# The first k in two hardware transfers, and the identity built on POOL behind the third load

## The chip, the cores and the metric

One core of one Trainium2 chip. The metric is the device time of one execution, in microseconds (us). Engines are named as the profile names them: PE multiplies matrices (PEld is its weight load), DVE, ACT and POOL are the elementwise engines, and SP only issues transfers here. A transfer goes either through a "hardware" queue (issued on SP or ACT) or through the "software" queue (issued on POOL). A name ending in "q", as in POOLq, is the sequencer of that engine.

## The reference

```python
# q, k, v: (8, 12, 448, 64) f32; w_in: (768, 2048); w_out: (2048, 768)
scores = q @ k.transpose(0, 1, 3, 2) / sqrt(64)
attn   = np.maximum(scores, 0.0) ** 2 / 448
x      = (attn @ v).transpose(0, 2, 1, 3).reshape(3584, 768)
h      = x @ w_in
out    = (0.5 * h * (1 + erf(h / sqrt(2)))) @ w_out
```

## The kernel before

The kernel works through eight batches of twelve heads; a batch is three head groups of four. For the first batches, q and k are transposed on PE against an identity matrix. From batch 2 on, DVE packs them (`pk`, `pq`) and transfers issued on SP transpose them (`kT`, `qT`). All instructions go out in a recorded order, so that no engine chooses at run time.

The start: the first k and q come as f32 through two hardware queues, the identity is made by DVE and POOL, and PE spins on zeros until data come.

```python
    nc.scalar.dma_start(k32, kv_view(k, 0, 0, 1))
    nc.sync.dma_start(q32, q_view(0, 0, 1, 0, HC))
    zero = const.tile([128, 128], BF16, tag="zero", name="zero")
    V.memset(zero, 0.0)
    V.memset(ident, 0.0)
    nc.gpsimd.affine_select(
        out=ident, in_=ident, compare_op=mybir.AluOpType.not_equal, fill=1.0,
        base=0, pattern=[[-1, 128]], channel_multiplier=1,
    )
    # ... a warming activation on ACT ...
    for _ in range(SPIN):                      # 45
        nc.tensor.matmul(spin[:, 0, :128], zero, zero, start=True, stop=True)
```

The gate: a POOL instruction that copies one column of each of the four transposed parts of q. Its purpose, as the code reads, is to hold POOL, which issues the large loads, until the transposes of the batch have landed.

```python
        def fn(e):
            nc.gpsimd.tensor_copy(gate, get_T(b)[0][:, 0, ::KC])
```

Behind the gate of batch 2 stand the second and third load of `w_out` and then the next loads of k and q:

```python
    def load_wout(kf):
        w = moe_w_out.rearrange("(kf p) d -> p kf d", p=128)
        nc.gpsimd.dma_start(wout_sb[:, kf, :], w[:, kf, :])
```

Of the kernel before, what the change touches and what calls it, by code (L numbers as in the profile page):

```python
# [12 lines left out]
B, H, S, D = 8, 12, 448, 64  # L13
# [5 lines left out]
NK = S // KB  # L19
# [37 lines left out]
K_CUT = 4  # L57
# [1 line left out]


ORDER = """
G0 G1 G2 G3 G4 G5 A10 D13 G6 A16 P11 P14 G7 D12 A15 P17 G8 D18 P21 P39 D22 P33 P36 A34 D40
P19 D20 A37 P23 G9 P42 P48 D24 P54 A43 D35 A49 P51 D44 P25 D38 A52 D41 G117 A55 D53 P45 D50
A26 D47 A46 P57 D56 P69 P66 A58 D70 P27 G118 A67 P29 D59 P63 G119 A28 D71 P60 A64 G120 D68
P78 D61 A62 P75 A79 D65 P81 P31 D30 A76 D80 P96 G121 D32 A97 P72 D77 G122 A82 D98 P129 G123
# [140 lines left out]
def kernel(  # L206
# [9 lines left out]
    nc = tc.nc  # L216
# [24 lines left out]
    k32 = natpool.tile([128, 2, NK * D], F32, tag="pk", name="k32")  # L241
# [9 lines left out]
    def q_view(b, g0, g1, c0, c1):  # L251
        qq = q[b, 4 * g0 : 4 * g1].rearrange("h (p c) d -> p h (c d)", c=NC)
        return qq[:, :, c0 * D : c1 * D]
# [7 lines left out]
    def kv_view(t, b, g0, g1):  # L261

        return t[b, 4 * g0 : 4 * g1].rearrange("h s d -> (h s d)").rearrange(
            "(x p f) -> p x f", p=128, f=NK * D
        )
# [27 lines left out]
    ident = const.tile([128, 128], BF16, tag="ident", name="ident")  # L293
# [10 lines left out]
    V, A = nc.vector, nc.scalar  # L304
# [12 lines left out]
    sch = Scheduler({"w": 3, "a": NA, "f": 2, "osb": 3})  # L317
# [412 lines left out]
    def f2(b):  # L730
        tiles = range(0, 3) if b % 2 == 0 else range(3, 7)
        return [(2.6, add_f2(b // 2, t, n)) for t in tiles for n in range(2)]

    def mix(a, b):

        a, b = list(a), list(b)
        r, n = [], len(a) + len(b)
        na = len(a)
        for i in range(n):
            if a and (not b or (na - len(a) + 1) * n <= (i + 1) * na):  # L740
                r.append(a.pop(0))
            else:
                r.append(b.pop(0))
        return r
# [12 lines left out]
    def slots(first, last):  # L757
# [10 lines left out]
        return out + [[("AV", done)]]  # L768


    nc.scalar.dma_start(k32, kv_view(k, 0, 0, 1))
    nc.sync.dma_start(q32, q_view(0, 0, 1, 0, HC))
    zero = const.tile([128, 128], BF16, tag="zero", name="zero")
    V.memset(zero, 0.0)  # L774
    V.memset(ident, 0.0)
    nc.gpsimd.affine_select(
        out=ident, in_=ident, compare_op=mybir.AluOpType.not_equal, fill=1.0,
        base=0, pattern=[[-1, 128]], channel_multiplier=1,
    )
    warm = const.tile([128, 1], F32, tag="warm", name="warm")  # L780
    V.memset(warm, 0.0)

# [127 lines left out]
    x1, x2 = f1(B - 1), f2(B - 2)  # L910
    for _, o in x2[:1] + mix(x1, x2[1:]) + f2(B - 1):
        pe_q.append(o)
    sch.run({"PE": pe_q, "POOL": pool_q})
# [1 line left out]
_INS = ['q', 'k', 'v', 'moe_w_in', 'moe_w_out']  # L915
# [26 lines left out]
```

## Time and profile before

| what | value |
|---|---|
| time | 392.37 us, median of 3 runs (392.07 to 392.56) |
| span of the profiled run | 391.1 us |
| PE busy | 381.2 us (97%) |
| ACT, DVE, POOL busy | 200.1, 189.9, 45.7 us |
| first transposes on PE | 6.02 us |
| last landing that holds PE back | 86.3 us |

PE bounds the kernel over the whole.

The transfer queues, too, can be read from the page (packets, MB, share of 16 engines):

```profile
q10 hardware_dynamic: 304, 0.48, 0.3%
```

This is the queue of the first k: 256 of its packets are k (1792 bytes each), and 16 of 4 bytes tell that the transfer is complete. The other 32 belong to a small store that ACT issues at the end of the kernel. The q beside it is on another hardware queue.

### The profile page before, as it was taken

To read this page: it belongs to the slowest core of one execution; us is meant where nothing else is said; L and a number is where in the kernel's file an instruction comes from. 1 tells how busy PE (TensorE), PEld (TensorE's weight loads), DVE (VectorE), ACT (ScalarE), POOL (GpSimd) and SP (SyncE) were. 2 spreads that over 40 slices of the span, in tenths; PEclk is the share of its full clock that TensorE was granted. 3 is DMA by queue.
4 is the path that set the end of the run, shared out by engine and by line. 5 is a ranking of instruction groups with operands and counts; after the bars stand their busy time and mean duration, and the time that the engine had idled before them with its cause. 6 is when DMAs were issued, how large, how long until landed. Compare 5 with 4: busy or idle time off the path is not lost.

```text
span 391.1 us, 7974 instructions
## 1 busy us (share of the span) xinstructions
PE 381.2 (97%) x3437; PEld 211.6 (54%) x3437; DVE 189.9 (49%) x350; ACT 200.1 (51%) x304; POOL 45.7 (12%) x69
## 2 busy tenths in 40 slices
PE   8799999998999999999999999999999999999996
PEld 7576554454555555555555555555555555555563
DVE  3999952457636444644555346545355352110121
ACT  4988855743536554565734466366536645222200
POOL 8665304000200200020000200000000000000000
PEclk9999999999999999999999999999999999999999
DMA  9999998999997691689129961380112011100132
GB/s 176 195 203 204 197 175 112 210 202 152 182 188 134 126 178 42 130 138 169 42 65 159 128 125 42 76 148 2 40 23 60 2 42 40 42 13 29 40 80 82
DMA packets 69523, 42.94 MB, mean 110 GB/s; under 512 B 37744, under 2 KB 65904, under 8 KB 69488
## 3 DMA queue, kind: packets, MB, share of 16 engines
q0 software_dynamic: 30512, 22.47, 38.4%
q1 hardware_dynamic: 38672, 19.49, 24.1%
q8 instruction: 27, 0.44, 0.5%
q10 hardware_dynamic: 304, 0.48, 0.3%
q14 instruction: 8, 0.07, 0.0%
HBM read 45.61 MB, written 11.01 MB: 145 GB/s over the span
## 4 chain that ended last, share of the span: by engine, by line
PE 85%; DMA 7%; DVE 4%; SPq 1%; ACT 1%; POOL 1%; issue 0%; POOLq 0%
PE pso L687 36%; PE psh L644 33%; PE ps L535 8%; PE pav L597 7%; DMA nq<-in_q_dram 5%; DVE a_sq L556 2%; SPq L498 1%; DMA q<-in_q_dram 1%; DVE a_sq L549 1%; DMA qT<-pq 1%; ACT a_sq L547 1%; PE tp L465 1%; PE tp L437 0%; DVE osb L308 0%; DVE pq L397 0%
## 5 line engine op out<-in xcount | busy, mean ns | idle before, releaser
L644 PE MATMUL psh<-xT,win_sb 128*128 128x448 bf16 (+1 forms) x804 | 154.3, 344 | 0.0
L687 PE MATMUL pso<-wout_sb,h_sb 128*128 128x384 bf16 (+2 forms) x896 | 151.7, 326 | 0.6 <-DVE osb L308 0.6
L547 ACT ACTIVATE a_sq<-ps 128x896 bf16<-128x896 f32 (+1 forms) x141 | 123.2, 914 | 48.9 <-PE ps L535 48.8
L556 DVE TENSOR_TENSOR a_sq<-a_sq 128x896 bf16<-128x896 bf16 (+1 forms) x169 | 100.5, 618 | 53.7 <-ACT a_sq L547 53.5
L656 ACT ACTIVATE h_sb<-psh 128x448 bf16<-128x448 f32 x128 | 70.0, 547 | 98.5 <-PE psh L644 98.5
L687 PEld LDWEIGHTS <-h_sb 128*128 128x128 bf16 x896 | 86.2, 98 | 63.0 <-issue 6.3
L644 PEld LDWEIGHTS <-win_sb 128*128 128x128 bf16 x804 | 76.2, 98 | 70.4 <-issue 9.5
L308 DVE COPY osb<-pso 128x384 f32<-128x384 f32 (+2 forms) x56 | 31.2, 557 | 89.6 <-PE pso L687 89.6
L535 PE MATMUL ps<-qT,kT 64*64 64x448 bf16 (+1 forms) x756 | 47.0, 336 | 2.6 <-DVE a_sq L549 0.9
L549 DVE TENSOR_SCALAR a_sq<-ps 128x896 bf16<-128x896 f32 x28 | 30.4, 1090 | 35.9 <-PE ps L535 35.6
L597 PE MATMUL pav<-a_sq,v_sb 64*64 64x448 bf16 (+1 forms) x756 | 37.3, 330 | 1.0 <-ACT a_sq L547 0.4
L535 PEld LDWEIGHTS <-kT 64*64 64x64 bf16 x756 | 18.4, 105 | 24.2 <-issue 19.2
L597 PEld LDWEIGHTS <-v_sb 64*64 64x64 bf16 x756 | 21.3, 107 | 13.6 <-issue 2.9
L308 DVE CAST xT<-pav 128x448 bf16<-128x448 f32 (+1 forms) x29 | 16.3, 567 | 9.2 <-ACT xT L310 4.6
L310 ACT CAST xT<-pav 128x448 bf16<-128x448 f32 (+1 forms) x25 | 12.4, 495 | 15.5 <-PE pav L597 9.8
L510 POOL COPY gate<-qT 128x4 bf16<-128x4 bf16 x5 | 0.9, 187 | 157.4 <-DMA qT<-pq 157.4
L257 POOL DMA_DIRECT2D nq<-in_q_dram x14 | 11.6, 829 | 2.0 <-DMA win_sb<-in_moe_w_in_dram 0.8
L359 POOL DMA_DIRECT2D v_sb<-in_v_dram x14 | 10.6, 759 | 2.6 <-DMA win_sb<-in_moe_w_in_dram 2.0
L341 POOL DMA_DIRECT2D nk<-in_k_dram x13 | 10.0, 768 | 5.5 <-DVE xT L308 2.2
L397 DVE COPY pq<-nq 112x512 bf16<-112x512 bf16 x36 | 8.2, 287 | 1.5 <-DMA nq<-in_q_dram 1.5
L386 DVE COPY pk<-nk 128x896 bf16<-128x896 bf16 x18 | 6.3, 386 | 1.8 <-DMA nk<-in_k_dram 1.8
L787 PE MATMUL spin<-zero 128*128 128x128 bf16 x45 | 4.8, 306 | 1.0 <-DVE zero L774 1.0
(26 smaller groups left out, 44.0 us busy)
## 6 DMA issues: line engine op xcount, KB each, us to landing
nk<-in_k_dram POOLq DMA_DIRECT2D x5, 672.0 KB, 9.0
nq<-in_q_dram POOLq DMA_DIRECT2D x5, 672.0 KB, 10.9
v_sb<-in_v_dram POOLq DMA_DIRECT2D x5, 672.0 KB, 13.9
out_dram<-osb SPq DMA_DIRECT2D x7, 336.0 KB, 2.8
wout_sb<-in_moe_w_out_dram POOLq DMA_DIRECT2D x2, 1152.0 KB, 11.4
out_dram<-osb SPq DMA_DIRECT2D x8, 288.0 KB, 2.7
v_sb<-in_v_dram POOLq DMA_DIRECT2D x9, 224.0 KB, 9.0
out_dram<-osb SPq DMA_DIRECT2D x8, 240.0 KB, 2.8
```

The source lines that it names most:

```text
L257: nc.gpsimd.dma_start(nq[b][:, 4 * g0 : 4 * g1, c0 * D : c1 * D], q_view(b, g0, g1, c0, c1))
L308: V.tensor_copy(dst, src)
L310: A.copy(dst, src)
L359: nc.gpsimd.dma_start(vt[b][:, 2 * g0 : 2 * g1], kv_view(v, b, g0, g1))
L535: nc.tensor.matmul(ps[64 * j : 64 * j + 64, e, x * w : x * w + w], kT[r, g, i * 128 + 64 * j : i * 128 + 64 * j + 64], qT[r, 2 * g + j, co ...
L547: A.activation(ar, ps, AF.Relu, scale=c_att)
L549: V.tensor_scalar(ar, ps, c_att, 0.0, op0=mybir.AluOpType.mult, op1=mybir.AluOpType.max,)
L556: V.tensor_mul(box["a2"][:, :, :used], ar, ar)
L597: nc.tensor.matmul(pav[0][o2 : o2 + 64, e, :w], vt[b][r, 2 * g + e, bass.ts(i, D)], box["a2"][r, e, o : o + w], start=(i == 0), stop=(i == ...
L644: nc.tensor.matmul(ph[:, x * n : x * n + n], win_sb[:, kd, bass.ts(m + x, 128)], xT[b][:, kd, c], start=(kd == 0), stop=(kd == KD - 1),)
L656: A.activation(hT[b // 2][:, m : m + nm, o + c.start : o + c.stop], box[0][:, :S].rearrange("p (x n) -> p x n", x=nm), AF.Gelu,)
L687: nc.tensor.matmul(po[:, :w], hT[pr][:, kf, bass.ts(t, 128)], wout_sb[:, kf, c], start=(kf == 0), stop=(kf == KF - 1),)
```

## The change

The intent was to have the first four of seven blocks of k, and q, land earlier, so that PE can begin, and to take the building of the identity out of the way of the first software loads.

```diff
@@ ORDER
-G0 G1 G2 G3 G4 G5 A10 D13 G6 ...
+G0 G1 G2 G1152 G3 G4 G5 A10 D13 G6 ...
@@
-    nc.scalar.dma_start(k32, kv_view(k, 0, 0, 1))
+    for i in (slice(0, K_CUT * D), slice(K_CUT * D, NK * D)):       # K_CUT = 4, NK = 7
+        nc.scalar.dma_start(k32[:, :, i], kv_view(k, 0, 0, 1)[:, :, i])
     nc.sync.dma_start(q32, q_view(0, 0, 1, 0, HC))
@@
-    V.memset(ident, 0.0)
-    nc.gpsimd.affine_select(
-        out=ident, in_=ident, compare_op=mybir.AluOpType.not_equal, fill=1.0,
-        base=0, pattern=[[-1, 128]], channel_multiplier=1,
-    )
@@
+    def fn_ident(e):
+        nc.gpsimd.memset(ident, 0.0)
+        nc.gpsimd.affine_select(...)           # as above
+
+    sch.add((("POOL", 0.4, 0.5),), fn_ident)
```

More of the change, by code (lines that the diff above doesn't have):

```diff
@@ L61 @@
 ORDER = """
-G0 G1 G2 G3 G4 G5 A10 D13 G6 A16 P11 P14 G7 D12 A15 P17 G8 D18 P21 P39 D22 P33 P36 A34 D40
+G0 G1 G2 G1152 G3 G4 G5 A10 D13 G6 A16 P11 P14 G7 D12 A15 P17 G8 D18 P21 P39 D22 P33 P36 A34 D40
 P19 D20 A37 P23 G9 P42 P48 D24 P54 A43 D35 A49 P51 D44 P25 D38 A52 D41 G117 A55 D53 P45 D50
@@ L912 @@
         pe_q.append(o)
+    def fn_ident(e):
+        nc.gpsimd.memset(ident, 0.0)
+        nc.gpsimd.affine_select(
+            out=ident, in_=ident, compare_op=mybir.AluOpType.not_equal, fill=1.0,
+            base=0, pattern=[[-1, 128]], channel_multiplier=1,
+        )
+    sch.add((("POOL", 0.4, 0.5),), fn_ident)
     sch.run({"PE": pe_q, "POOL": pool_q})
```

## The prediction

> **What bounds the kernel now.** The change touches only the first microseconds, so I read the page's groups first (PE is busy 381.2 of 391.1 us), then the chain of waits for the opening, then the timeline of each engine there, then the stretches by window, and last the packets and landings of single transfers. From 21.4 us on the chain is nearly all PE, back to back, apart from one transfer that holds it from 67 to 86 us and which is itself started by earlier work. So what happens before 21.4 us should shift everything behind it, and is otherwise worth nothing. The chain of the opening (start, length, what):
>
> ```profile
> 0.74 4.58 DMA q<-in_q_dram
> 5.33 0.02 issue
> 5.35 0.63 ACT nq L310
> 5.97 0.04 issue
> 6.02 0.39 PE tp L465 x8
> ...
> 6.71 0.59 ACT kT L310
> 7.30 0.04 issue
> 7.35 0.40 PE tp L465 x8
> 7.75 0.02 issue
> 7.77 0.39 DVE qT L308
> 8.16 1.08 DVE a_sq L549
> 9.24 0.60 PE tp L437 x14
> 9.84 0.02 issue
> 9.87 0.62 DVE kT L308
> ```
>
> By this view the time starts with the landing of the first q (5.33), goes through its cast and transposes, and reaches the elementwise work that keeps DVE full until 17.5. The reader should not trust it at 9.24. The timeline of the weight loads says of the same 14 transposes (start, length, engine, line, operation, and in brackets the idle time and its releaser):
>
> ```profile
> 8.40 0.42 PEld L437 LDWEIGHTS <-nk 128*64 128x64 bf16 x14 [0.17 <-issue]
> 9.24 0.42 PEld L437 LDWEIGHTS <-nk 128*64 128x64 bf16 x14 [0.42 <-DMA nk<-in_k_dram]
> 9.75 0.56 PEld L535 LDWEIGHTS <-kT 64*64 64x64 bf16 x21
> ```
>
> These are the transposes of the k of head group 2. Nothing in the code makes them wait for a squaring step; their PSUM buffer was free at 8.16, when DVE had copied qT. Their k comes over the software queue, issued on POOL at 3.80 and landed 5.4 us later, at 9.20. So at 9.24 the landing of that transfer and not the chain through q is what holds PE, and two things wait behind it: the DVE copy of kT at 9.87 (all later DVE work is in order behind it), and the scores of the following steps at 9.75, for which ACT waited until 10.09. DVE came free at 9.77, only 0.10 us ahead, so the two paths are nearly level.
>
> Is that transfer limited by its issue or by the engines? The stretches (first columns: window, length, PE; the last two are the mean busy share of the transfer engines and GB/s):
>
> ```profile
> 1.75:3.00 1.25, 1.25 (x15) 1.25 (x14) 0.00 (x0) 0.98 (x2) 1.16 (x3) 1.00 0.35 92
> 3.00:4.50 1.50, 1.50 (x17) 1.50 (x16) 0.00 (x0) 0.00 (x0) 1.50 (x4) 1.00 1.08 374
> 4.50:6.00 1.50, 1.27 (x14) 1.10 (x12) 0.45 (x1) 0.65 (x2) 1.50 (x4) 1.00 1.37 201
> 6.00:9.30 3.30, 2.71 (x70) 2.00 (x72) 2.48 (x6) 1.93 (x4) 3.30 (x5) 1.00 1.42 196
> ```
>
> From 3.0 us the engines are never idle (the shares over 1 are overlapping packets; the 200 GB/s of the software queue are bytes written, half of those it reads). The issue is far ahead: POOL issued this k at 3.80 and its packets ran from about 7.7 to 8.85. What sets 9.20 is therefore the sum of bytes and packets ahead of it.
>
> **What the Trainium skill says.** "DMA: Bandwidth & Descriptors", section Issuing engines are not separate DMA queues: all queues share the same 16 engines, and starting on several saves only issue time. The trace agrees: the share above stays over 1 from 3.0 us on whoever issued. Its section Queues, rings and completion order says that an engine goes round-robin between the queues with work. Here the trace agrees in part: q (512-byte packets) and k (1792-byte) alternate nearly one to one from 3.0 to 4.3 us (40 and 44 in the quarter from 3.75), but the software queue's first packet starts at 4.37, as the first engine finishes both hardware transfers, although it was issued at 1.24 and an issue into idle engines (64.42) shows its first packet 1.5 us later. Its section Anatomy of one DMA puts most of the fixed cost after the last byte; here q's last packet ends at 4.73 and it lands at 5.33, so 0.6 us.
>
> **The change part by part.** (1) k in two. Same 448 KB, but 256 packets of 1024 bytes and 256 of 768 in place of 256 of 1792. A 512-byte packet takes 27 ns and a 1792-byte one 74, which gives 0.037 ns a byte and 8 ns a packet; from the software queue's packet rates (57 of 1792 bytes read, 173 of 512, in a quarter microsecond over 16 engines) the fixed part comes to 4.5 ns. Sixteen more packets on each engine are 0.07 to 0.13 us of work more, all ahead of the software queue. The benefit: a pair of q packet and k packet takes about 27 + 46 = 73 ns in place of 101, so 16 pairs from 3.0 us end near 4.2 and not 4.6; q and the first four blocks should land about 0.4 us earlier, near 4.9 and 5.1; the last three blocks near 5.6 (estimate, if the software queue still waits).
>
> (2) What that buys. ACT casts q 0.4 us earlier, but PE is spinning until 5.77 (45 matmuls from 0.99, 4.78 us, unchanged). So the first transposes move from 6.02 to about 5.79: at most 0.23 us, whatever the landing. The copies and scores follow: DVE would come free at about 9.54 in place of 9.77.
>
> (3) What meets it. The k of group 2 lands at 9.20 + 0.07 to 0.13 = 9.27 to 9.33. Its transposes start at 9.31 to 9.37, end 0.58 later, and DVE copies kT at 9.94 to 10.00 in place of 9.87; ACT's third activation likewise. The 0.23 us gained is spent waiting here, and the stage goes on 0.1 us late.
>
> (4) The identity. DVE loses a memset of 0.11 us at 0.90, when it has 4.5 us idle ahead: worth nothing. POOL's 0.31 us selection moves from behind the first load to behind the third, with a memset of perhaps 0.1 to 0.2 us (the page's four small ones take 0.10 each). The second and third load are issued 0.33 us earlier, the fourth about 0.15 later; with packets queued for 3 us and more neither is seen. The identity is ready at about 4.0, before PE needs it at 5.77. A second issue on ACT costs about 0.47 us at 1.21, which pushes the table load to end near 3.0, before the cast. The program order of all else should stay: the recorded order is a list, and one word is put in it.
>
> Sum: +0.07 to +0.13 us on the path, no gain left. From 21.4 us PE is full and simply shifts; the transfer that holds it to 86 us is started by a gate that shifts too, and the transfer stream before it is longer by the same 0.1.
>
> **The rivals.** A: the gain passes through. If the transposes at 9.24 did wait for DVE as the chain says, or the software queue's k landed no later, PE's 0.23 us would reach the end: 392.1 to 392.2. For it: the chain's own words, and that DVE and the transfer are within 0.1 us of one another. Against: the weight load's releaser, and full engines. B: the last three blocks come late. If the software queue does take its turn while they are under way, from about 4.2 us each of their 16 packets per engine waits for a 70 ns one: 16 x (36 + 70) = 1.7 us, last packet near 5.9, landing near 6.5. ACT casts until 7.0, its copy of kT, which stands behind that cast in order, ends at 7.6 and not 7.30, and the chain above starts 0.3 us late: 392.7. For it: round-robin later on (47 to 55 us, transposes and loads alternate). Against: the late first packet at 4.37. C: nothing moves, because the engines have slack before 3.0 us (share 0.35) that takes up the additional packets: 392.4. Against: that idle time lies before the k packets come at all.
>
> **Range and chances.** I take my sum at about 45%, C at 25%, A at 20% and B at 10%. From 392.37 that gives a centre of 392.45. The three runs before spread over 0.5 us, so a median may be off by 0.15; with A and B as the ends the range is 392.0 to 392.9. Two per cent would be 7.8 us; nothing here is of that size, short of a changed order or a transfer that stalls, so the outer chances are about one in a hundred or less.
>
> **What would show each step.** q's cast should start near 4.9 on ACT and the first four blocks' cast near 5.1 on DVE; the first transposes at 5.78 to 5.85, no earlier, right behind the spin. The second part's packets should be of 768 bytes and the software queue's first one at about 4.4 to 4.5. The wait to look for is the weight load of group 2's k: its idle time should grow from 0.42 to 0.6 us or more, with the landing at 9.27 to 9.33, and DVE's copy behind it should show an idle gap of about 0.3 us where it has 0.10. The PE start of the full stretch, 21.41 before, should be 21.4 to 21.55. The prediction is wrong if that start moves by more than 0.2 us either way, if group 2's transposes start before 9.2, or if ACT's second cast starts after 6.3.

## More of the kernel before

The transposing transfers of a batch: three of k, then four of q, one after the other on SP.

```python
        for c in range(NC):                    # 4
            def fn(e, c=c):
                nc.sync.dma_start_transpose(get_T(b)[0][:, :, bass.ts(c, KC)], get_p()[0][:, c, :])
```

The chain of waits around the gate of batch 2 (start, length, what) reads in the kernel before:

```profile
61.44 2.69 DMA qT<-pq
64.13 0.05 issue
64.18 0.19 POOL gate L510
64.37 0.05 issue
64.42 0.46 POOL wout_sb L280
...
67.15 19.17 DMA nq<-in_q_dram
86.32 0.02 issue
86.34 1.30 DVE pq L397 x6
```

The last transposing transfer lands at 64.13, the gate runs, the `w_out` load is issued 0.29 us after the landing, and the q of batch 3 is issued behind it at 67.15. It lands at 86.32, and DVE packs it. In the stretch around that landing PE is not full. The row below has the window, its length and PE's busy time first:

```profile
80.00:92.00 12.00, 10.23 (x98) 5.42 (x96) 8.28 (x20) 6.33 (x9) 0.00 (x0) 1.00 1.42 190
```

PE is idle for 1.77 of these 12 us.

## The result and the profile after

| kernel | median | lowest to highest | runs |
|---|---|---|---|
| before | 392.14 us | 391.93 to 392.56 | 6 |
| after | 392.92 us | 392.24 to 393.89 | 6 |

The ratio is 1.0021, with a 95% interval of 1.0005 to 1.0037. A ratio here is the mean time of one kernel's fast runs over that of the other's of the same rounds, so it is not quite the ratio of the medians quoted beside it. The class "within 2%" is right. The time of 392.92 lies just above the range that ended at 392.9, and the step from the kernel before (0.82 us between the means) is ten times the 0.08 that was predicted. All outputs are right.

The first thing the profile says is that it does not contain this step: both profiled runs have a span of 391.1 us. So the two traces can show what each part did, but the cost of 0.8 us has to be found by more runs. The queue of the first k now has 272 packets more: 256 of k, as the prediction counted, and 16 of 4 bytes that tell that one more transfer is complete:

```profile
q10 hardware_dynamic: 576, 0.48, 0.4%
```

The stretches of the opening, as in the prediction (the last two columns are the share of the transfer engines and GB/s):

```profile
1.75:3.00 1.25, 1.25 (x15) 1.25 (x14) 0.00 (x0) 1.22 (x1) 1.25 (x3) 1.00 0.67 144
3.00:4.50 1.50, 1.50 (x17) 1.50 (x16) 0.00 (x0) 0.38 (x3) 1.42 (x4) 1.00 1.12 353
```

The share before 3.0 us is 0.67 where it was 0.35. The first packet runs at 1.77 us in both kernels, but more of them ran before 3.0. The timeline of the engines in the kernel after (start, length, engine, line, operation, and in brackets the idle time and its releaser):

```profile
4.40 0.62 ACT L310 CAST nq<-q 112x512 bf16<-112x512 f32 x1 [1.11 <-DMA q<-in_q_dram]
4.64 0.43 DVE L308 CAST nk<-k 128x512 bf16<-128x512 f32 x1 [3.70 <-DMA k<-in_k_dram]
5.20 0.51 ACT L310 CAST nk<-k 128x384 bf16<-128x384 f32 x1 [0.18 <-DMA k<-in_k_dram]
5.88 0.39 PE L465 MATMUL tp<-ident,nq 112*64 112x112 bf16 x8
...
9.23 0.42 PEld L437 LDWEIGHTS <-nk 128*64 128x64 bf16 x14 [0.55 <-DMA nk<-in_k_dram]
...
9.86 0.62 DVE L308 COPY kT<-tp 128x896 bf16<-128x896 bf16 x1 [0.23 <-PE tp L437]
```

The cast of q starts at 4.40 and not at 5.35, that of the first four blocks of k at 4.64 and not 5.55. (Over all traces of this document the cast of q starts between 4.31 and 5.21 in the eight kernels with k in two, and between 5.11 and 5.54 in the ten with k in one, so the split brings it forward, mostly by less than here.) PE starts its transposes at 5.88 and not 6.02. All of that is lost at 9.23: the weight load of group 2's k waits 0.55 us where it waited 0.42, and starts at the same place as before (9.24). DVE copies behind it at 9.86 (before: 9.87) with a gap of 0.23 us. In this pair of traces the opening gives nothing, and no cost shows.

Next comes a landing that varies from trace to trace (the transposes behind it started between 19.92 and 21.15 in the traces with the usual spin): the first k of batch 1 lands at 20.59, and PE's transposes of it start at 20.63 in place of 20.10. The scores that started at 21.41 before start at 21.55, and the next scores and the first product with `w_in` are 0.31 us late (22.87 in place of 22.56). This lateness is not the change's: in two further traces of the kernel before (e4_before_again, e16_before_again) that product starts at 22.89 and 22.80. At the end of the trace it is gone. The chain of waits at the gate:

```profile
61.20 2.70 DMA qT<-pq
63.91 0.03 POOLq L510
63.94 0.10 issue
64.04 0.18 POOL gate L510
64.22 0.27 issue
64.48 0.45 POOL wout_sb L280
...
67.33 19.05 DMA nq<-in_q_dram
86.38 0.02 issue
86.40 1.30 DVE pq L397 x6
```

Here is the one thing in the trace that nothing in the diff seems to touch. The last transpose lands at 63.91, which is 0.22 us earlier than before. Yet the load behind the gate is issued at 64.48, 0.06 us later than before. From landing to issue it takes 0.57 us where it took 0.29.

### The profile page after: what moved, and what is told of

The parts are those of the page before. It is cut to its first block, busy times and chain, and to the rows that moved or that the text cites. A ratio compares the mean times of both kernels' runs of the same rounds, so it can differ in the third digit from the quotient of the medians.

```text
span 391.1 us, 7974 instructions
## 1 busy us (share of the span) xinstructions
PE 381.0 (97%) x3436; PEld 211.7 (54%) x3437; DVE 189.7 (49%) x349; ACT 200.4 (51%) x304; POOL 45.8 (12%) x70
## 4 chain that ended last, share of the span: by engine, by line
PE 84%; DMA 9%; POOL 2%; DVE 1%; SPq 1%; issue 1%; ACT 1%; POOLq 0%
PE pso L687 36%; PE psh L644 33%; PE ps L535 8%; PE pav L597 7%; DMA nq<-in_q_dram 5%; DMA nk<-in_k_dram 2%; DMA v_sb<-in_v_dram 1%; SPq L498 1%; DMA qT<-pq 1%; POOL nk L341 1%; DVE a_sq L556 0%; POOL v_sb L359 0%; DVE osb L308 0%; DVE pq L397 0%; POOL wout_sb L280 0%
```

## The experiments

**Theories.** The first: the 0.28 us at the gate is real, caused by the change, and reaches the end, because the load behind it is what PE waits for at 86 us. A listing of the compiled instructions gives a reason. The gate of batch 2 waits on four completion semaphores, which count the landing of a transfer (HW0 to HW7 are eight, which the hardware transfers take in turn, in program order). Shortened to the names:

```
before   gate<-qT 128x4   waits HW6, HW7, HW5, HW0
after    gate<-qT 128x4   waits HW6, HW7, HW1, HW0
```

Before, two loads come first, then the three transposes of k take HW2 to HW4 and the four of q HW5, HW6, HW7 and HW0: the part that lands last is on the semaphore that is waited on last. After, three loads come first, and the four of q are on HW6, HW7, HW0 and HW1: the part that lands last is on HW1, which now stands third, and a wait on HW0, which was complete 1.32 us before (62.59 against 63.91), comes behind it. In the listing the first three waits are in two separate semaphore instructions ahead of the gate, and only the fourth is in the gate itself. The listing comes from compiling the kernels and not from the chip; the two traces agree with it on the fourth wait. The rivals: the identity on POOL costs the time (its memset and a later fourth load); the lateness of PE in the opening, of whatever origin, passes to the end; the smaller packets of the split cost it; or the 0.8 us is mostly chance.

**The change again, and each part alone (same chip, same rounds).** The kernel after once more; the kernel before with the split alone; with the identity alone; and the kernel before once more, to see how far two copies of one kernel lie apart.

```diff
# e2_split_only: before, with
-    nc.scalar.dma_start(k32, kv_view(k, 0, 0, 1))
+    for i in (slice(0, K_CUT * D), slice(K_CUT * D, NK * D)):
+        nc.scalar.dma_start(k32[:, :, i], kv_view(k, 0, 0, 1)[:, :, i])
# e3_ident_only: after, with
-    for i in (slice(0, K_CUT * D), slice(K_CUT * D, NK * D)):
-        nc.scalar.dma_start(k32[:, :, i], kv_view(k, 0, 0, 1)[:, :, i])
+    nc.scalar.dma_start(k32, kv_view(k, 0, 0, 1))
# e1_after_again and e4_before_again: unchanged copies
```

> The changed kernel once more, to see whether its 0.8 us over the kernel before come back. Theory 1 (the opening is held by the landing of group 2's k, everything else is noise of single runs): within 0.2 us of the kernel before, ratio 1.000 to 1.0005. Theory 2 (the change makes later loads land late in many runs): 0.4 to 1.0 us over it again, and a spread of single runs over 1 us.

> k in two transfers, identity as before. If the split is the cause of the loss, this is as slow as the changed kernel (+0.4 to +1.0 us); if the identity is, it equals the kernel before within 0.2 us. In the profile, q should be cast at about 4.4 and group 2's k land at 9.2 in any case.

> Identity on POOL behind the third load, k in one transfer. If the split is the cause of the loss, this equals the kernel before within 0.2 us; if the identity is (a memset and a selection of 0.24 and 0.29 us ahead of the fourth load's issue), it loses 0.4 us or more. In the profile q should be cast at about 5.35 as before and group 2's k land at 9.2.

> The kernel before against itself: the noise of the comparison. Ratio 1.000 with an interval under 0.0005 either side if single runs spread by 0.6 us, as its six did. If it is itself 0.5 us off or spreads over more than 1 us, the 0.8 us of the changed kernel is within the noise.

| run | median | lowest to highest | ratio (95%) | landing to `w_out` issue |
|---|---|---|---|---|
| before | 392.80 | 391.53 to 394.17 (11 runs) | | 0.29 (its own trace) |
| e1_after_again | 392.92 | 392.33 to 394.80 | 1.0015 (0.9992 to 1.0037) | 0.58 |
| e2_split_only | 393.13 | 392.81 to 394.48 | 1.0015 (0.9995 to 1.0035) | 0.58 |
| e3_ident_only | 392.60 | 391.51 to 393.23 | 0.9993 (0.9973 to 1.0012) | 0.29 |
| e4_before_again | 392.49 | 391.57 to 393.40 | 0.9995 (0.9975 to 1.0014) | 0.29 |

No difference is clear by itself, and the two copies of the kernel before show why: their medians are 0.31 us apart. But the order is that of the first theory, and the gate divides the four without exception: 0.58 us with the split, 0.29 without it. The identity alone shows no loss, so the rival that blames it has nothing for it.

**The order of the waits, with and without the split.** If the number of hardware loads at the start is what counts, one tiny load more, and k unsplit, must show 0.57. And the split with seven tiny loads more (ten loads in all, so two and eight) must show 0.29.

```diff
# e5_one_tiny: before, with
     nc.sync.dma_start(q32, q_view(0, 0, 1, 0, HC))
+    tiny = const.tile([16, 4 * 1], F32, tag="tiny", name="tiny")
+    for i in range(1):
+        nc.sync.dma_start(tiny[:, 4 * i : 4 * i + 4], k[0, 0, 0:16, 4 * i : 4 * i + 4])
# e6_split_seven_tiny: e2_split_only, with
-    q32 = natpool.tile([KC, 4, HC * D], F32, tag="pq", name="q32")
+    q33 = natpool.tile([KC, 5, HC * D], F32, tag="pq", name="q32")
+    q32 = q33[:, :4]
     nc.sync.dma_start(q32, q_view(0, 0, 1, 0, HC))
+    for i in range(7):
+        nc.sync.dma_start(q33[0:16, 4, 4 * i : 4 * i + 4], k[0, 0, 0:16, 4 * i : 4 * i + 4])
```

> The kernel before, k in one transfer, with one more hardware transfer of 256 bytes behind q, which nobody reads. It only shifts the eight completion semaphores of the hardware queues by one, so that POOL's gate waits for the four transposes in the order that the split kernels have. Theory G (the split costs through that order): from the landing of the last transpose to the issue of the next load 0.57 us, as in the three profiles with the split, and not 0.29, as in the three without; the median up by 0.3 us or so. Rival S (the split itself, its packets or its place in the stream): 0.29 us, and equal to the kernel before.

> k in two transfers, and seven more transfers of 256 bytes, so that the semaphores are back in the order of the kernel before (ten hardware transfers ahead of the transposes in place of two). Theory G: landing to issue 0.29 us again, and the time that of the kernel before within its noise, 0.3 us or so under the split alone. Rival S: 0.57 us stays, or the time stays 0.8 us over.

The chain at the gate, first of the kernel with one tiny load:

```profile
60.62 2.74 DMA qT<-pq
63.36 0.03 POOLq L510
63.39 0.10 issue
63.49 0.19 POOL gate L510
63.68 0.27 issue
63.94 0.46 POOL wout_sb L280
```

and of the split with seven tiny loads:

```profile
61.41 2.71 DMA qT<-pq
64.12 0.05 issue
64.18 0.19 POOL gate L511
64.36 0.05 issue
64.41 0.46 POOL wout_sb L281
...
66.06 0.60 issue
```

The first goes from landing to issue in 0.58 us, the second in 0.29. The compiled waits are HW6, HW7, HW1, HW0 in the first, and HW6, HW7, HW5, HW0 in the second. So the rotation of the semaphores is the cause of this 0.29 us, and the size of k's packets is not. The gates on fewer parts, further below, show the same of the order by itself. How the order costs it is not shown: the traces have a piece of the sequencer and a 0.10 us gap ahead of the gate, and a gap of 0.27 in place of 0.05 behind it.

The times (medians 392.76 and 392.94 beside 392.41 of before; ratios 1.0011, 0.9995 to 1.0028, and 1.0014, 1.0000 to 1.0029) separate nothing. For the second I had expected the time of the kernel before, and that was a miss. In its trace the third load behind the gate, the next k, was held 0.60 us where it was held 0.25 (the last line above), but from the issue of `w_out` to the packing only about 0.14 us of that is left (22.07 against 21.92). So the trace does not explain the longer time. It is a good test of the gate; in time, it does not speak for the gate as the only cost.

**Does a late opening reach the end?** PE's spin was lengthened, so that the opening comes late by a known amount.

```diff
-SPIN = 45
+SPIN = 55      # e7_spin55
+SPIN = 75      # e9_spin75
```

> The kernel before with 55 spinning matmuls in place of 45, which hold PE to 6.8 us and delay the opening by 0.7 to 0.8 us. The prediction's step (from 21.4 us everything shifts by what the opening loses): +0.7 to +0.8 us. The rival that the six profiles suggest (the end is 304.74 us after batch 3's q is there, and the transfers set that): under +0.3 us, with the shift of 0.7 us to be seen at 21 us and gone at 91.

> The kernel before with 75 spinning matmuls: 55 delayed nothing, because PE's faster half came earlier in that run, so this one adds 30, some 1.6 us at 55 ns, and the first transposes should start near 7.0 and the opening be 0.5 to 1.4 us late at 21 us. The prediction's step (all shifts): as much longer at the end. The rival (transfers set the end): under 0.3 us, with batch 3's q landing at about 86.3 and the end 304.7 us after it.

The run with 55 was a miss: ten spins more moved the first transposes from 6.02 to 5.87. The spins took 107 ns each up to about 4.3 us and 56 ns from there. In other traces this change of pace came at another time, or not before the spin was over, so 45 spins ended anywhere from 4.97 to 5.98 us. The Trainium skill ("TensorE: Matmul & The Clock Gate", Part 1) gives the same two steps for such matmuls, and says that the moment varies between runs; this case agrees, with a wider variation (last section). Its time (median 392.90, ratio 1.0011, 0.9994 to 1.0029) says nothing about a delay, as there was none.

With 75 the delay came. The timeline of PE:

```profile
0.99 6.76 PE L787 MATMUL spin<-zero 128*128 128x128 bf16 x75 [0.99 <-DVE zero L774]
7.68 0.39 PE L465 MATMUL tp<-ident,nq 112*64 112x112 bf16 x8
```

PE's first transposes are 1.66 us late, and the first transposing transfer of batch 2 is issued at 44.98 in place of 42.74. But the last of them is issued at 61.58 in place of 61.44, the gate is 0.16 late, q of batch 3 lands 0.52 late, and the end of the trace is at 391.65 in place of 391.10, so 0.55 late. The stretch where PE waited reads:

```profile
80.00:92.00 12.00, 11.53 (x116) 6.20 (x107) 9.49 (x23) 6.47 (x9) 0.00 (x0) 1.00 1.45 182
```

PE idles 0.47 us here and not 1.77. A late PE has more work left when it comes to this wait, and waits less. The runs agree: median 393.31 beside 392.82, ratio 1.0014 (0.9998 to 1.0030), a mean 0.48 us longer. The interval ends at 1.2 us, so the full 1.66 does not come through; it does not exclude that nothing does. Of the 0.52 us at q's landing only 0.16 were there at the gate, and the rest came in the loads behind it (from the issue of `w_out` to the packing 22.28 us against 21.92; other traces with the unchanged gate have 21.92 to 22.22). So about two thirds of this delay, or more, are absorbed. The few tenths by which PE was late in the changed kernel can't be the 0.8 us. Both of my expectations missed: the delay did not come through whole, and the end was not within 0.3 us.

What does set the end is the packing of batch 3's q. From its start to the end of the trace it takes the same time in kernels that reach it differently:

| trace | `pq` starts | end | difference |
|---|---|---|---|
| before | 86.34 | 391.10 | 304.76 |
| after | 86.40 | 391.09 | 304.69 |
| e2_split_only | 87.89 | 392.62 | 304.73 |
| e3_ident_only | 85.93 | 390.67 | 304.74 |
| e9_spin75 | 86.86 | 391.65 | 304.79 |
| e15_second_on_sp (below) | 88.28 | 393.00 | 304.72 |

The other traces lie between 304.67 and 304.80 too, with one exception (e12_gate_two_again), which comes next.

**Move the gate.** If the landing behind the gate sets the end, a gate that opens earlier must bring the end forward by as much, until PE is full. The gate of batch 2 was made to wait for only two of the four transposes, or for one. The code uses the gate only as a delay, and the results stayed right.

```diff
         def fn(e):
-            nc.gpsimd.tensor_copy(gate, get_T(b)[0][:, 0, ::KC])
+            n = 2 if b == 2 else NC            # n = 1 in e10_gate_one
+            nc.gpsimd.tensor_copy(gate[:, :n], get_T(b)[0][:, 0, : n * KC : KC])
# e8_gate_two and e12_gate_two_again: before with this; e11_after_gate_two: after with this
```

> The kernel before, with POOL's gate of batch 2 reading two of the four transposed pieces of q in place of four, so that the loads behind it are issued 1 to 2 us earlier. If the gate sets the end (theory of the transfers): 0.5 to 1.5 us faster. If the opening sets it: no change. What may eat the gain: the last two transposes share the engines with the loads, and PE's scores at 64.8 us need them.

> Gate of batch 2 on the first piece of q alone, with a single wait. If the transfers set the end, the loads are issued another 0.6 us and, with no second wait to pass, 0.3 us earlier than with two pieces: 0.5 to 1.0 us under that kernel, 390.5 to 391.0. If the transposes behind it now hold up PE's scores at 64.8, the gain shrinks to nothing.

> The changed kernel (split and identity) with the gate on two pieces. In this pair the waits of the gate stand in the same order with and without the split, and single runs spread by 0.3 us and not 0.7. Theory G (the split costs by the order of the gate's waits alone): equal to the unchanged kernel with this gate within 0.2 us. Rival S (another cost of the split, some 0.4 us left after the 0.29): 0.3 to 0.6 us over it.

> The kernel before with the gate on two pieces, for comparison on the same chip: 0.7 to 1.1 us faster than the kernel before, as in the last set.

| run | median | before, same rounds | ratio (95%) | `w_out` issued | `pq` starts | end |
|---|---|---|---|---|---|---|
| e8_gate_two | 391.45 | 392.41 | 0.9972 (0.9957 to 0.9987) | 62.32 | 84.97 | 389.76 |
| e10_gate_one | 392.02 | 392.82 | 0.9990 (0.9958 to 1.0021) | 62.32 | 85.90 | 390.69 |
| e11_after_gate_two | 391.52 | 392.82 | 0.9978 (0.9952 to 1.0005) | 62.84 | 84.69 | 389.37 |
| e12_gate_two_again | 390.99 | 392.82 | 0.9951 (0.9936 to 0.9966) | 61.96 | 84.10 | 389.12 |

The timeline of POOL and the stretch where PE had waited, both of the second copy on before:

```profile
61.51 0.18 POOL L511 COPY gate<-qT 128x2 bf16<-128x2 bf16 x1 [17.33 <-DMA qT<-pq]
61.96 1.65 POOL L280 DMA_DIRECT2D wout_sb<-in_moe_w_out_dram  x2 [0.27 <-issue]
```

```profile
80.00:92.00 12.00, 12.00 (x113) 6.66 (x112) 10.16 (x23) 7.20 (x9) 0.00 (x0) 1.00 1.31 179
```

The load is issued 2.46 us earlier than before, the packing starts 2.24 us earlier, PE has no idle time left in this stretch, and the trace ends 1.98 us earlier. From `pq` to the end it now takes 305.02 us, 0.2 to 0.3 more than in all other traces: PE is full and has become what sets the end. In the first copy (e8_gate_two) the load is issued 2.10 us earlier and the trace ends 1.34 earlier. This is the strongest proof here: the gate sets the time, by most of its amount. The kernel is also faster than the kernel before, by 0.3% and 0.5% in its two sessions, with intervals that leave out 1; the second gain, 2.0 us between the means, is nearly double what I had expected. It spreads little (0.70 and 0.55 us from lowest to highest, where before spreads 1.8 and 1.9 in the same sessions).

These gates also test the order of the waits, in kernels whose opening is as before. With two parts the compiled list is HW6, HW5: the part that lands later is waited on first, in a semaphore instruction of its own. From its landing to the load it then takes 0.59 us in e8_gate_two and in e12_gate_two_again, and 0.59 with the split (e11_after_gate_two, HW7, HW6). With one part there is a single wait, in the gate itself, and it takes 0.29 (62.03 to 62.32 in e10_gate_one). The chain of e8_gate_two:

```profile
57.20 4.54 DMA qT<-pq
61.73 0.02 issue
61.76 0.02 POOLq L511
...
62.05 0.27 issue
62.32 0.46 POOL wout_sb L280
```

With one transpose the gate did not do better. Its runs went from 390.86 to 394.58. In its trace the first part landed at 62.03, so the load was issued at 62.32, no earlier than in e8_gate_two, where the second part had landed at 61.73. From that issue to the packing it took 23.58 us, where before took 21.92. That the loads and the remaining transposes hinder one another would be an obvious reason, but the transposes don't show it (2.06 us from the first part's landing to the last's, against 2.51 before), and why the loads took longer was not settled.

On the changed kernel the gain is there as well (391.52), but one run of 394.15 makes the interval wide. This run was also meant as a test of whether the split costs anything beside the order, which is the same there: equal to e12_gate_two_again within 0.2 us if not, 0.3 to 0.6 over it if so. Its median is 0.53 over it in the same rounds (the means 0.93, or 0.47 without the run of 394.15). That speaks for a second cost, but with six timings that spread over 3.2 us against five it does not show one.

**What is left of the 0.8 us.** The gate's 0.29 us is about a third of the 0.82 us measured first. The last session split k in other ways, to see whether the split costs more.

```diff
# e13_split_again: a copy of e2_split_only; e16_before_again: a copy of before
# e14_two_equal: before, with two transfers that keep the packets at 1792 bytes
-    nc.scalar.dma_start(k32, kv_view(k, 0, 0, 1))
+    for i in range(2):
+        nc.scalar.dma_start(k32[:, i], kv_view(k, 0, 0, 1)[:, i])
# e15_second_on_sp: before, with the second part behind q on SP
-    nc.scalar.dma_start(k32, kv_view(k, 0, 0, 1))
+    nc.scalar.dma_start(k32[:, :, : K_CUT * D], kv_view(k, 0, 0, 1)[:, :, : K_CUT * D])
     nc.sync.dma_start(q32, q_view(0, 0, 1, 0, HC))
+    nc.sync.dma_start(k32[:, :, K_CUT * D :], kv_view(k, 0, 0, 1)[:, :, K_CUT * D :])
```

> The split alone, once more: with the gate's order it is 0.29 us slower. If there is another cost of some 0.4 us, the mean is 0.6 to 0.8 us over the kernel before; if the rest was noise, 0.2 to 0.4.

> k in two transfers cut the other way, so that each keeps 128 packets of 1792 bytes. The gate's order is that of the split (+0.29 us). If the smaller packets cost the rest, this is 0.2 to 0.4 us over the kernel before; if a third transfer or ACT's additional instruction does, 0.6 to 0.8.

> The split with its second part on SP's queue, behind q: ACT's program is as long as before. If ACT's additional instruction costs the rest, 0.2 to 0.4 us over the kernel before; if the packets do, 0.6 to 0.8.

> The kernel before against itself on the same chip: within 0.3 us of it; if further off, means of six runs can't settle 0.4 us.

| run | median | lowest to highest | ratio to before, 392.76 (95%) | landing to `w_out` issue |
|---|---|---|---|---|
| e13_split_again | 392.81 | 391.89 to 393.08 | 0.9997 (0.9984 to 1.0011) | 0.58 |
| e14_two_equal | 392.61 | 392.14 to 396.22 | 1.0008 (0.9979 to 1.0037) | 0.58 |
| e15_second_on_sp | 392.92 | 392.54 to 394.85 | 1.0005 (0.9990 to 1.0020) | 0.57 |
| e16_before_again | 392.70 | 392.29 to 393.48 | 0.9999 (0.9985 to 1.0012) | 0.29 |

All three splits show the 0.57 to 0.58 us at the gate, as a third hardware load must. None is measurably slower than before here. The split alone came out with a mean 0.05 us under before, below both of my expectations, so not even the gate's 0.29 is seen in its time, and two sizes of packet and two queues for the second part differ by nothing that stands out.

Taken together, the four runs with the split of the change (the changed kernel twice, the split alone twice, 24 timings) are slower than the kernels of the same sessions without it (before and its copies and the identity alone, 46 timings) by 0.82, 0.78 and -0.06 us in the three sessions. Weighted by the number of timings that is 0.55 us, with a standard error of 0.15 (one timing scatters by 0.60 us around the mean of its session and group). The gate accounts for 0.29 of it. The other 0.26 is under two standard errors, and its session-to-session scatter is larger than that. With e6_split_seven_tiny and e11_after_gate_two on one side and this last session on the other, whether it is chance or a second cost of the split stays open.

The scatter itself has a place in the traces. Where a trace ended late (392.6 and 393.0 us), the last transpose had landed late (65.13 and 65.66 us, where it landed between 63.3 and 64.5 in the other traces with the unchanged gate), and everything behind the gate came late with it. What makes that landing vary between runs of one program was not settled.

## Why the prediction was right or wrong

**What holds PE at 9.24: right.** The weight load's releaser was the better witness than the chain of waits. The transposes were ready 0.13 us earlier and started at the same place, so the opening's gain was spent there. (This is so in the pair that was predicted. In two other traces, e2_split_only and e12_gate_two_again, PE did not wait for this landing.)

**(1) The split's packets: size off.** Group 2's k was to land at 9.27 to 9.33. It landed at 9.19, as before (9.20). The rival that gave the engines slack before 3.0 us was right about this step: their share there rose from 0.35 to 0.67 and the last hardware packet came at 4.64 and not 4.82. The expected 0.07 to 0.13 us of cost does not show. A cost of that size is below the scatter, though: these transposes start between 9.13 and 9.50 in five traces with the split of the change, and between 9.12 and 9.90 in nine with k in one (that with 75 spins left out). The casts came 0.5 us earlier than I had put them (4.40 against 4.9 for q, 4.64 against 5.1 for k). The rival that let the last three blocks come late is refuted: ACT's second cast started at 5.20. One reading of the prediction is off: in the quarter from 3.75 the page counts 44 packets of q and 44 of k, not 40 and 44; nothing rests on it.

**(2) The gain on PE: right, with a wrong floor.** The first transposes moved from 6.02 to 5.88, 0.03 past the latest that I had expected (5.85). "No earlier than the end of the spin" holds, but the spin's end is no fixed 5.77: in the second profile of the same kernel the transposes began at 5.46.

**(3) What meets it: right in kind.** The gain is spent in waiting, and the stage goes on at 9.86 where it went on at 9.87 (predicted 9.94 to 10.00).

**(4) The identity: right.** The memset took 0.24 and the selection 0.29 us on POOL (predicted 0.1 to 0.2 for the memset), the fourth load was issued 0.25 us later (predicted 0.15), and neither was seen; the identity alone lost nothing.

**The step that failed** is the end of the working: "From 21.4 us PE is full and simply shifts; the transfer that holds it to 86 us is started by a gate that shifts too". PE was not full (1.77 us idle from 80 to 92), and a delay ahead of it does not simply shift: of 1.66 us at the first transposes, at most 0.55 reached the end. The prediction's own test, PE's start at 21.41, came out at 21.55 and so within its bounds; but it tested nothing, since the same PE is 0.31 us late one microsecond later, as it is in copies of the kernel before, and nothing of that is seen at the end. I had seen the transfer of 19 us in the chain, but took its start to move with PE. It moves with the last transposing transfer, and that hardly moved with PE where this was tried (in the run with 75 spins the first transposing transfer was issued 2.24 us late and the last 0.14).

**The term that was missing** is beside it, in "The program order of all else should stay". The order did stay. But one hardware load more turned the rotation of completion semaphores by one, and the gate of batch 2 then took 0.57 us from the last landing to the load behind it in place of 0.29. The sum had +0.10 for an opening in which no cost showed, and nothing for a gate that cost 0.29. In the two traces laid side by side it is hidden by a landing that happened to be 0.22 us earlier.

**The range was too narrow.** It took the spread of three runs (0.5 us) for the scatter. Over the sessions, of which the later four were on four different chips, the medians of the kernel before ran from 392.14 to 392.82, and two copies of it had 392.49 and 392.70. The time of 392.92 is 0.02 us above the range; of the 0.82 us between the means of that session the runs explain 0.29, and the rest is not told apart from chance. By so small a margin the time could as well have fallen inside.

## What to carry to other kernels

Look for the last wait of the engine that bounds the kernel, and judge a change by what it does to the chain in front of that wait; a gain or loss earlier than that was mostly absorbed here. When a change adds a transfer anywhere, compare the compiled waits of the instructions that gate later transfers, since their semaphores and their order can change although no line of theirs did. And run the unchanged kernel twice as two entries before explaining a difference of 0.2%.

## What the Trainium skill lacked or had wrong

- No page that I found says what the order of the waits costs when one POOL instruction waits on several completion semaphores. Here the time from the last landing to the load behind the gate was 0.57 to 0.58 us in seven traces with the order HW6, HW7, HW1, HW0 and 0.28 to 0.29 in seven with HW6, HW7, HW5, HW0; with two waits, the later landing first, 0.59 in three, and with a single wait 0.29 in one. "Perfetto Trace Analysis", section Identifying Dependency Chains, says that an instruction waiting on several engines may have separate semaphore instructions put in front of it; the piece of POOLq of 0.03 us ahead of the gate agrees with that, but the page gives no cost.
- "DMA: Bandwidth & Descriptors", section Queues, rings and completion order, has each engine go round-robin between its queues. At the start, the software queue's first packet ran at 4.37 us in the kernel before and at 4.06 in the kernel after, each time as the first engine had finished its hardware packets, though it was issued at 1.24. What holds it there no page says.
- "TensorE: Matmul & The Clock Gate", Part 1, is right on the two paces of a spin (107 and 56 ns here) and warns that their moment varies. It puts the change of pace around 4 us into the activity, give or take 0.5; here it came 2.8 us (e5_one_tiny) to 5.1 us (e9_spin75) after the first spin. So a spin of 45 ended anywhere from 4.97 to 5.98 us, and one of 55 at 5.81.
